# A windowed-attention and token-mixing kernel: the written-out order of all its work, replaced by a newly searched one

## The chip, the cores and the metric

One core of a Trainium2 chip. The metric is the time of one execution on the device, in microseconds (us), of which the median over runs is given. The engines that matter are TensorE (PE, with its weight loads PEld), VectorE (DVE), ScalarE (ACT), GpSimd (POOL) and the queue SP, which issues the DMA transfers. Each engine works through its own list of instructions in order and waits on semaphores for the others.

## The reference

Two branches work on the same x of 2048 tokens by 512 features, and a gate mixes them.

```python
x = A_x
g = sigmoid((x * gate_w).sum(-1, keepdims=True))
# A: attention, 32 heads of 16, each token sees itself and the 255 before it
q, k, v = split(x @ wqkv)
p = softmax(where(0 <= i - j < 256, q @ k.T / 4, -1e9))
a = (p @ v).reshape(S, D) @ wo
# B: layernorm over features, then an MLP over the tokens
h = layernorm(B_x)                      # B_x holds the same x here
u = gelu(h.T @ w1 + b1)                 # 512 x 1376
b = (u @ w2 + b2).T                     # 2048 x 512
out = g * a + (1 - g) * b
```

Scores, exponentials and products are in bfloat16 with sums in float32.

## The kernel before

**Tiles.** The tokens stand in 16 tiles of 128 (j = 0 to 15); scores are worked on in blocks of 128 queries that start half a tile late, so that a window of 256 needs two full blocks of keys (A, B) and two half-size corners (C).

**Tasks.** The program first writes down 1115 tasks. A task has a name, the engines that may run it with a cost in us for each, the tasks it waits for, and the buffers it takes and gives back. The names say what they do; a point and a number count pieces of one chain of matmuls:

- `q`, `k`, `v`: projections. `k3_2` is key group 3 of the third quarter of the tokens; `v12` is the values of tile 12. `qc`, `kc`, `vc` copy them out of PSUM. The quarters of x arrive transposed: the first by TensorE (`xta`, copied by `xtc`), the others by transposing DMAs (`xt1`, `xt2`, `xt3`).
- `s10.v1`: a score visit, 8 or 16 matmuls of 32 rows (line L942) into two pairs of PSUM banks; `s10.C`: a corner visit (L1043). `e10.v1.0` is ACT's exponential of one pair (L894), `m10.v1.0` its mask, a multiplication on DVE (L907, L974) or a selection on POOL (L536). `pv10.0` to `.3` multiply by the values (L1088), with four column tiles of 32. `n110`, `n210`, `nz10`, `n310`, `n410` normalise on DVE and put the result back into `xo`.
- `bs`, `ba`, `pow`, `h`: layernorm. `u0` to `u10`: the first layer of the MLP in chunks of 128 of the 1376; `ub` adds the bias. `gelu` is one task on ACT that works on all of u in four slices, between two loads of ACT's function table. `y0` to `y15`: the second layer and, as its last four matmuls, the output projection of the attention, in one accumulation; `f` applies gate and bias, `o` writes out.
- On SP: `x`, `wqk`, `wv`, `w1`, `w2`, `wo` load; `vs` and `vz` copy pieces of v to other partitions, so they wait for `vc`.

**What sets the order.** `PLAN` (L190) holds one string for each engine: the names in the order in which this engine runs them. After a colon stand the places of the buffers that a task takes, such as the two PSUM bank pairs of a score visit. So both which engine does a task and when is written out, and nothing moves at run time. A task whose turn has come holds up everything behind it on its engine.

`arrange` (L85) walks through these lists with the costs and gives each task a planned start. The plan is emitted in the order of these starts; they decide little else: a few waits between DVE and POOL where both use a port close in time, and the emission of a DMA among the others.

**Tiling of TensorE.** The array works either whole, or split into tiles of fewer rows or columns: mode `d` whole, `s` 32 by 128 (score visits), `c` 32 by 64 (corners), `p` 128 by 32 (products with the values), `h` 64 by 32. Pieces of the chains `q`, `k`, `v`, `u`, `y` are flexible: behind a task named in `THEN` they are written as four column tiles each, in mode `p`, and otherwise whole. Every piece of a chain is two matmuls of 512 columns, or eight when split.

Of the kernel before, what the change touches and what calls it, by code (L numbers as in the profile page):

```python
# [78 lines left out]
SWITCH = 0.095  # L79

BLOCK, AHEAD, FETCH, BUSY = 256, 80, 3.6, 3.0
LATENCY = {"PE": 0.22, "ACT": 0.15, "DVE": 0.12, "POOL": 0.15, "SP": 2.0}


def arrange(tasks):  # L85
# [21 lines left out]
    while len(order) < len(tasks):  # L107
# [19 lines left out]
        t.cost = t.engines[e]  # L127
        ins = t.ins
        if e == "PE":
            new = then if t.flex else t.mode  # L130
            if new != mode:
                t.cost += SWITCH
            if t.flex and new == "p":
                t.tiled = True
                ins *= 4
            if t.mode != "d":
                then = "p" if t.name in THEN else "d"
            mode = new
# [52 lines left out]
        warm:3 xta0.0.0:7 xta0.0.1:6 warmb xta0.1.1:4 xta0.1.0:5 q1_0.0:2 k3_0.0:3 k1_0.0:6 q3_0.0:1 k0_0.0:7  # L191
        q3_0.1 q0_0.0:0 k3_0.1 q1_0.1 q1_0.2 k1_0.1 k3_0.2 k0_0.1 q0_0.1 q2_0.0:5 q1_0.3 q0_0.2 q1_0.4 q0_0.3
        k3_0.3 q3_0.2 q0_0.4 k3_0.4 q3_0.3 k2_0.0:4 q2_0.1 k0_0.2 k1_0.2 k1_0.3 k0_0.3 k1_0.4 q2_0.2 q3_0.4 q2_0.3
        k0_0.4 k2_0.1 k2_0.2 k2_0.3 k2_0.4 q2_0.4 s0.v0:62 q3_1.0:0 q3_1.2 k3_1.0:1 k3_1.2 q0_1.0:7 s0.C:42 v1.0:6
        q0_1.2 s-1.C:02 v1.2 v2.0:5 v2.2 s1.v3:02 biast:4 v0.0:7 v0.2 v3.0:5 v3.2 q1_1.0:4 s1.v0:62 v5.0:1 q1_1.2
        gate0:5 v5.2 v14.0:0 s0.v1:62 v13.0:5 k2_1.0:1 v14.2 pv-1.0:6 v10.0:4 k2_1.2 v13.2 s1.v2:26 k2_2.0:0 v10.2
        v15.0:1 v12.0:5 v12.2 v15.2 k2_2.2 pv0.0:2 pv0.1 s1.v1:64 pv0.2 v4.0:1 v4.2 k3_2.0:0 k3_2.2 s2.v1:26 v7.0:5
        v7.2 k0_2.0:4 s1.C:60 k0_2.2 v6.0:3 v6.2 s2.v3:06 k0_1.0:2 k0_1.2 k1_1.0:5 k1_1.2 pv1.0:6 pv1.1 pv1.2
        s2.v0:02 v11.0:4 v11.2 v8.0:5 v8.2 pv1.3 pv1.4 s2.v2:20 q2_1.0:5 v9.0:4 q2_1.2 s2.C:26 v9.2 k1_2.0:1 k1_2.2
        u3.0:0 u3.2 s3.v1:64 u3.4 u3.6 u3.8 s3.C:26 u3.10 u3.12 u3.14 u2.0:1 s3.v2:24 pv2.0:6 pv2.1 u7.0:0 pv2.2  # L200
        pv2.3 u7.2 u2.2 s3.v0:42 u2.4 u7.4 u7.6 s3.v3:46 u7.8 u7.10 u7.12 s4.v0:62 u2.6 u2.8 u2.10 u2.12 u2.14
        s4.v1:24 pv3.0:6 pv3.1 pv3.2 pv3.3 u7.14 u10.0:1 u10.2 s5.v2:42 u10.4 u10.6 u10.8 s4.v3:62 u10.10 q0_2.0:0
        q0_2.2 s4.v2:64 u10.12 u10.14 q3_2.0:2 u0.0:3 q3_2.2 s4.C:06 u0.2 u0.4 u0.6 s6.v0:40 u0.8 u0.10 u0.12
        u6.0:2 u0.14 s5.v0:06 pv4.0:4 pv4.1 pv4.2 pv4.3 u6.2 u6.4 q2_2.0:3 s5.v1:06 u6.6 q2_2.2 u6.8 s5.C:64 u6.10
        u6.12 u5.0:3 s6.C:60 u6.14 u5.2 u5.4 s6.v2:46 u5.6 k3_3.0:2 k3_3.2 q1_2.0:1 q1_2.2 u5.8 s5.v3:46 u5.10
        u1.0:2 u1.2 s6.v1:06 u1.4 pv5.0:4 u5.12 pv5.1 pv5.2 pv5.3 s6.v3:06 u1.6 u5.14 u1.8 s7.v0:64 u1.10 pv6.0:0
        pv6.1 pv6.2 u1.12 pv6.3 s7.v1:64 u1.14 u4.0:3 u4.2 s7.v3:06 u4.4 k1_3.0:2 k1_3.2 s7.C:04 u4.6 u4.8 q0_3.0:2
        s7.v2:60 q0_3.2 u4.10 u4.12 u4.14 s8.v3:46 u9.0:2 u9.2 u9.4 s8.C:04 u8.0:3 u8.2 u8.4 u8.6 s8.v1:46 u8.8
        u9.6 u9.8 s8.v0:04 u8.10 u9.10 u9.12 u8.12 u8.14 s8.v2:06 pv7.0:4 u9.14 pv7.1 pv7.2 pv7.3 s10.v0:02
        k0_3.0:7 k0_3.2 q1_3.0:4 q1_3.2 q3_3.0:6 k2_3.0:5 k2_3.2 q3_3.2 pv8.0:0 pv8.1 pv8.2 pv8.3 y4.0:3 q2_3.0:6  # L210
        q2_3.2 y0.0:7 y0.2 y0.4 y8.0:2 y0.6 y4.2 y0.8 s9.v1:40 y4.4 y8.2 y0.10 y8.4 y0.11 y0.13 s9.v3:40 y4.6 y4.8
        y4.10 y4.11 s9.v2:60 y4.13 y8.6 y8.8 s9.C:04 y7.0:3 y8.10 y7.2 y8.11 s9.v0:60 y7.4 y8.13 y7.6 s10.C:46 y7.8
        y2.0:2 y2.2 s10.v3:06 y2.4 y7.10 y2.6 y7.11 s11.v3:46 y2.8 y7.13 pv9.0:0 pv9.1 pv9.2 pv9.3 s10.v2:64 y2.10
        y2.11 y9.0:3 y9.2 s10.v1:04 y2.13 y9.4 y9.6 s11.C:60 y9.8 y1.0:2 y1.2 s11.v2:40 y1.4 y1.6 y9.10 y1.8
        s11.v1:06 y9.11 y9.13 y1.10 y1.11 s13.v3:04 y1.13 pv10.0:6 pv10.1 pv10.2 pv10.3 s12.v2:02 y5.0:5 y10.0:4
        y10.2 s12.v0:26 y5.2 y10.4 y5.4 y10.6 s11.v0:06 y5.6 y5.8 y5.10 y5.11 s12.v1:02 y10.8 y10.10 y10.11 y5.13
        s12.v3:62 y10.13 pv11.0:0 pv11.1 pv11.2 y3.0:5 pv11.3 s13.v0:26 y3.2 y11.0:4 y11.2 s12.C:60 y3.4 y11.4
        y11.6 s13.C:62 y11.8 y11.10 y11.11 y3.6 s13.v1:20 y11.13 pv12.0:6 y3.8 pv12.1 pv12.2 pv12.3 s14.v3:20 y3.10
        y3.11 y6.0:4 y3.13 s13.v2:26 y6.2 y6.4 y12.0:5 s14.v2:06 y12.2 y12.4 y6.6 s14.v0:02 y6.8 y6.10 pv13.0:6
        pv13.1 pv13.2 y6.11 pv13.3 s14.v1:02 y12.6 y12.8 y6.13 s14.C:26 y12.10 y12.11 y12.13 y13.0:0 y14.0:1 y14.2  # L220
        y13.2 s15.A:62 pv14.0:4 pv14.1 y14.4 pv14.2 pv14.3 y13.4 s15.C:26 y14.6 y13.6 y13.8 s15.B:42 y15l.0:7 y14.8
        y15l.2 y15r.0:6 y15l.4 y15l.6 y13.10 pv15.0:4 y14.10 pv15.1 pv15.2 y15r.2 y15l.8 y15l.10 y15r.4 y13.11
        y14.11 y14.13 y13.13 y15r.6 y15r.8 y15l.11 y15l.13 y15r.10 y15r.11 y15r.13
    """,
    ACT="""
        xtc0.0.1 xtc0.1.0 xtc0.1.1 kc3_0 kc1_0 kc0_0 kc2_0 e0.v0.0:4 e0.v0.1:5 kc3_1 e0.C.1:8 e0.C.0:a e-1.C.1:7
        e-1.C.0:b vc1 vc2 e1.v3.1:2 e1.v3.0:3 vc3 e1.v0.0:6 e1.v0.1:9 vc5 gatee0 e0.v1.0:d e0.v1.1:c vc14 kc2_1
        vc13 e1.v2.1:b e1.v2.0:7 vc12 vc15 kc2_2 e1.v1.0:5 e1.v1.1:a vc4 e2.v1.1:4 e2.v1.0:8 e1.C.1:d e1.C.0:c vc7
        vc6 e2.v3.1:1 e2.v3.0:0 kc1_1 e2.v0.1:a e2.v0.0:9 vc8 vc11 e2.v2.0:b e2.v2.1:5 e2.C.1:e vc9 e2.C.0:f
        e3.v1.0:c e3.v1.1:d e3.C.0:7 e3.C.1:6 ub3 e3.v2.0:a e3.v2.1:4 e3.v0.0:b e3.v0.1:5 e3.v3.1:f e3.v3.0:e  # L230
        e4.v0.1:1 e4.v0.0:0 e4.v1.0:b e4.v1.1:4 ub7 e5.v2.1:f e5.v2.0:e e4.v3.0:a e4.v3.1:d e4.v2.0:5 ub10
        e4.v2.1:c e4.C.0:2 e4.C.1:3 e6.v0.1:9 e6.v0.0:8 gatee1 e5.v0.1:0 e5.v0.0:1 e5.v1.1:c e5.v1.0:d e5.C.0:4
        e5.C.1:5 e6.C.0:7 e6.C.1:6 e6.v2.1:a e6.v2.0:b kc3_3 e5.v3.1:g e5.v3.0:h e6.v1.0:2 e6.v1.1:3 gatee2
        e6.v3.1:g e6.v3.0:h e7.v0.0:f e7.v0.1:e ub5 e7.v1.0:g e7.v1.1:d e7.v3.0:h e7.v3.1:c e7.C.0:9 e7.C.1:8
        e7.v2.0:a e7.v2.1:b e8.v3.0:6 e8.v3.1:7 e8.C.1:3 e8.C.0:4 e8.v1.0:2 e8.v1.1:5 e8.v0.0:1 e8.v0.1:0 gatee3
        e8.v2.0:f e8.v2.1:e e10.v0.0:g e10.v0.1:h gelu e9.v1.1:b e9.v1.0:8 e9.v3.1:9 e9.v3.0:2 e9.v2.1:4 e9.v2.0:3
        e9.C.0:5 e9.C.1:i e9.v0.0:a e9.v0.1:j e10.C.1:6 e10.C.0:f e10.v3.1:0 e10.v3.0:c e11.v3.0:1 e11.v3.1:d
        e10.v2.1:7 e10.v2.0:e e10.v1.0:5 e10.v1.1:4 e11.C.1:3 e11.C.0:j e11.v2.1:b e11.v2.0:a e11.v1.0:i e11.v1.1:2
        e13.v3.0:9 e13.v3.1:8 e12.v2.1:c e12.v2.0:0 e12.v0.1:f e12.v0.0:g e11.v0.0:5 e11.v0.1:e e12.v1.1:4
        e12.v1.0:7 e12.v3.0:h e12.v3.1:e e13.v0.1:d e13.v0.0:6 e12.C.0:1 e12.C.1:j e13.C.1:3 e13.C.0:i e13.v1.0:5  # L240
        e13.v1.1:2 e14.v3.0:j e14.v3.1:b e13.v2.1:c e13.v2.0:f e14.v2.0:e e14.v2.1:a e14.v0.1:7 e14.v0.0:d
        e14.v1.1:h e14.v1.0:i e14.C.0:f e14.C.1:g f12:0 e15.A.1:c e15.A.0:h e15.C.0:j e15.C.1:5 e15.B.0:9 e15.B.1:f
        f14:1 f15l:3
    """,
    DVE="""
        const zeros bs3:1 xtc0.0.0 bs2:0 ba3 parity bs1:1 ba2 ba1 bs0:0 ba0 qc1_0 bs4:1 qc0_0 ba4 qc3_0 qc2_0 qc3_1
        bs8:1 bs9:0 qc0_1 ba8 ba9 bs11:1 biasc vc0 bs5:0 ba11 ba5 bs10:1 bs7:0 ba10 ba7 gatem0 bs14:1 qc1_1 bs6:0
        n1-1:0 ba14 h2 n2-1 ba6 ez0 vc10 nz-1:0 bs12:1 n3-1:1 ba12 bs15:0 n10:0 h11 kc3_2 ba15 n20 h4 bs13:1 nz0:1
        h5 ba13 n30:0 h8 h1 m1.C.1 kc0_1 kc0_2 h6 h3 m1.C.0 h13 h14 h9 h7 n11:2 h10 h12 h0 h15 qc2_1 gl12 n21
        m2.C.1 kc1_2 m2.C.0 m2.v1.1 gl5 gl14 m3.C.0 gl15 n12:8 gl7 m3.v0.0 n22 m3.C.1 m3.v0.1 gl13 m3.v3.0 gl6 ub2  # L250
        gl10 gl4 nz2:0 nz1:1 n13:6 gatem1 gl8 gl11 gl9 n40 n4-1 qc0_2 n31:1 n32:0 qc3_2 m4.C.0 m4.C.1 n41 ub0 ez1
        n23 n14:2 m5.v0.0 nz3:1 m6.v0.1 qc2_2 m5.v2.1 n33:1 n24 m5.v0.1 gatem2 nz4:0 ub6 m5.C.1 m5.C.0 m5.v1.0 n43
# [36 lines left out]
def kernel(  # L289
# [139 lines left out]
    def add(*a, **k):  # L429
        tasks.append(Task(*a, **k))  # L430
        return tasks[-1]
# [944 lines left out]
```

## Time and profile before

| what | value |
|---|---|
| median of 3 runs | 200.1 us (199.95 to 200.97) |
| profiled execution: span from first to last instruction | 198.5 us |
| granted TensorE clock | 0.999 |
| matmuls | 4058 |
| PE busy | 193.7 us |
| ACT busy | 169.2 us |
| DVE busy | 156.5 us |
| POOL busy | 79.9 us |

The profile has the span alone; the runs are measured from outside, and their median lies 1.6 us above it. A row of a group or of the timeline has the line, the engine, the operation, what it writes and reads by the program's names, and how many instructions there were. `pb` is a single PSUM bank, `ps` a pair; `et` and `XT` hold exponentials (the latter in the space of the transposed x once it is used up), `wb` the weights of the MLP, `xo` x and later the attention's result. PE's ends are modelled, so the distance from one start to the next says more than the length of a row. Numbers in brackets behind a row are the idle time ahead of it, and who ended it.

### The profile page before, as it was taken

What the parts mean: (1) busy time and instruction counts of PE and PEld (TensorE: products, weight loads), DVE (VectorE), ACT (ScalarE), POOL (GpSimd) and SP (SyncE); (2) the same over time, 40 slices, a digit from 0 to 9 for tenths busy, and PEclk for the clock granted to TensorE, in tenths of its full rate; (3) what the DMA queues carried; (4) which work ended last, traced back from release to release, by engine and by line L of the source; (5) the groups of instructions that cost most, each with busy time, mean ns of one, the idle gap of its engine ahead of it and who ended that gap; (6) DMA issues with size and microseconds to landing.
All of it is one profiled execution on the core that took longest, in us unless ns stands there. A gap on an engine that the chain in (4) does not pass through costs nothing. (4 is left out here: it accounts for less than half of the span.)

```text
span 198.5 us, 9100 instructions
## 1 busy us (share of the span) xinstructions
PE 193.7 (98%) x4058; PEld 93.9 (47%) x4058; DVE 156.5 (79%) x318; ACT 169.2 (85%) x198; POOL 79.9 (40%) x118
## 2 busy tenths in 40 slices
PE   7999999999999999999999999999999999999993
PEld 3644444354535435446534554344445354554572
DVE  1799888879998988986689789636767868869683
ACT  2369999999987996998999899899899989898632
POOL 6394897425334440213223200055069335561310
PEclk9999999999999999999999999999999999999999
DMA  5999799990060000001499870000202220200002
GB/s 159 293 286 227 112 295 268 360 223 1 8 174 20 15 0 3 3 5 32 120 344 385 275 193 3 26 26 30 75 30 71 47 69 21 62 30 29 30 7 79
DMA packets 23189, 22.02 MB, mean 111 GB/s; under 512 B 7566, under 2 KB 21262, under 8 KB 23150
## 3 DMA queue, kind: packets, MB, share of 16 engines
q1 hardware_dynamic: 23150, 21.44, 38.3%
q8 instruction: 32, 0.52, 1.2%
q14 instruction: 7, 0.06, 0.1%
HBM read 15.61 MB, written 2.10 MB: 89 GB/s over the span
## 5 line engine op out<-in xcount | busy, mean ns | idle before, releaser
L894 ACT ACTIVATE et<-ps 128x1024 bf16<-128x1024 f32 (+1 forms) x94 | 89.4, 1013 | 6.1 <-PE ps L942 2.2
L536 POOL TENSOR_SCALAR_AFFINE_SELECT et<-et 128x512 bf16<-128x512 bf16 (+2 forms) x63 | 46.6, 751 | 56.0 <-ACT et L894 40.9
L894 ACT ACTIVATE XT<-ps 128x1024 bf16<-128x1024 f32 (+1 forms) x60 | 58.2, 1010 | 7.6 <-PE ps L942 4.4
L670 PEld LDWEIGHTS <-wb 128*32 128x32 bf16 (+4 forms) x645 | 32.0, 97 | 34.5 <-issue 6.5
L670 PE MATMUL pb<-ug,wb 128*32 128x512 bf16 (+4 forms) x385 | 45.6, 366 | 0.0
L670 PE MATMUL pb<-h,wb 128*128 128x512 bf16 (+2 forms) x260 | 44.5, 381 | 0.0
L536 POOL TENSOR_SCALAR_AFFINE_SELECT XT<-XT 128x512 bf16<-128x512 bf16 (+1 forms) x28 | 20.0, 720 | 46.8 <-ACT XT L894 27.8
L670 PE MATMUL pb<-XT,wqkv 128*128 128x512 bf16 (+2 forms) x190 | 32.8, 374 | 0.2 <-ACT XT L894 0.2
L1179 DVE STREAM_TRANSPOSE et<-ps 128x1024 f32<-128x1024 f32 (+1 forms) x17 | 20.1, 1183 | 12.0 <-PE ps L1088 11.3
L1088 PEld LDWEIGHTS <-VA 128*32 128x32 bf16 (+1 forms) x1056 | 20.1, 97 | 6.5 <-issue 1.3
L942 PE MATMUL ps<-QZ,KT 32*128 32x256 bf16 (+1 forms) x496 | 23.1, 265 | 0.0
L754 DVE TENSOR_TENSOR QZ<-pb,par 128x1024 bf16<-128x1024 f32 x16 | 19.5, 1219 | 3.2 <-PE pb L670 3.1
L670 PEld LDWEIGHTS <-wqkv 128*128 128x128 bf16 (+1 forms) x190 | 12.9, 99 | 14.3 <-ACT XT L894 0.5
L670 PE MATMUL pb<-wo,xo 128*32 128x512 bf16 (+2 forms) x152 | 18.0, 375 | 0.0
L1088 PE MATMUL ps<-et,VA 128*32 128x128 bf16 (+2 forms) x624 | 17.9, 218 | 0.0
L942 PEld LDWEIGHTS <-KT 32*128 32x128 bf16 x496 | 7.4, 92 | 20.6 <-ACT et L894 10.6
L670 PE MATMUL pb<-wqkv,XT 128*128 128x512 bf16 (+1 forms) x70 | 16.5, 381 | 0.0
L974 DVE TENSOR_TENSOR et<-et,mask 128x512 bf16<-128x512 bf16 x26 | 13.3, 510 | 2.5 <-ACT et L894 2.4
L441 DVE TENSOR_SCALAR ot<-pb,c,c 128x512 bf16<-128x512 f32 (+1 forms) x11 | 8.6, 783 | 7.4 <-PE pb L670 7.4
L1088 PE MATMUL ps<-XT,VA 128*32 128x128 bf16 (+2 forms) x432 | 13.9, 215 | 0.0
L1088 PEld LDWEIGHTS <-VZ 128*32 128x32 bf16 x832 | 13.2, 98 | 0.7
L770 DVE BATCH_NORM_STATS2 stats<-xo 128x6 f32<-128x512 bf16 x16 | 10.7, 682 | 3.1 <-DMA xo<-in_A_x_dram 3.1
(76 smaller groups left out, 200.1 us busy)
## 6 DMA issues: line engine op xcount, KB each, us to landing
wb<-in_B_w_dram SPq DMA_DIRECT2D x8, 512.0 KB, 7.6
wb<-in_B_w_dram SPq DMA_DIRECT2D x2, 2048.0 KB, 9.2
VZ<-VA SPq DMA_DIRECT2D x26, 70.0 KB, 2.7
xo<-in_A_x_dram SPq DMA_DIRECT2D x3, 512.0 KB, 6.3
out_dram<-ot SPq DMA_DIRECT2D x12, 128.0 KB, 2.0
wb<-in_B_w_dram SPq DMA_DIRECT2D x4, 352.0 KB, 5.9
wqkv<-in_A_wqkv_dram SPq DMA_DIRECT2D x4, 256.0 KB, 5.2
wb<-in_B_w_dram SPq DMA_DIRECT2D x1, 1024.0 KB, 5.3
```

Of the source, the lines that this page charges most:

```text
L441: return nc.vector.tensor_scalar(out=out_, in0=in_, scalar1=scale, scalar2=bias, op0=ALU.mult, op1=ALU.add)
L536: return nc.gpsimd.affine_select(out=out_, in_=in_, pattern=[[0, n] for n in pattern] + [[step, HB]], compare_op=op, fill=0.0, base=base_, ...
L670: made.append(nc.tensor.matmul(buf(b)[c:z_, c0:c0 + w_], lhsT=lhsT[:, c:z_], rhs=rhs, start=(j == 0), stop=(j == n - 1), skip_group_check= ...
L754: lambda k=k, b=b: nc.vector.tensor_tensor(out=QZ[:, k, :, (i % NQ) * SB:(i % NQ + 1) * SB], in0=buf(b)[:, None, :].to_broadcast([P, 2, SB ...
L770: f"bs{t_}", {"DVE": 0.67}, lambda b=b, t_=t_: nc.vector.bn_stats(buf(b)[:], xo[:, t_, :]),
L894: lambda e=e, b=b, shape=shape: nc.scalar.activation(out=shape(buf(e)), in_=shape(buf(b)), func=ACT.Exp, scale=SCALE),
L942: made.append(nc.tensor.matmul(to[:, :, done:done + m], lhsT=keys(j if x == "A" else j - 1, k)[rows], rhs=q[rows], start=True, stop=True, ...
L974: made.append(nc.vector.tensor_tensor(out=v, in0=v, in1=m.to_broadcast(list(v.shape)), op=ALU.mult))
L1088: return lambda: nc.tensor.matmul(to(), lhsT=v() if callable(v) else v, rhs=buf(e)[rows, col:col + n], start=first, stop=last, tile_positi ...
L1179: lambda: nc.vector.transpose(out=view(buf(tr).bitcast(FP32)), in_=view(buf(o))), [last], takes=[tr], uses=[o],
```

## The change

Two things change together.

The first is the costs in `arrange`: one price for every change of tiling becomes a table by kind, and a function corrects the costs of operations. The latencies, the time of an instruction fetch and the cost of `gelu` are lowered.

```diff
-SWITCH = 0.095
-BLOCK, AHEAD, FETCH, BUSY = 256, 80, 3.6, 3.0
-LATENCY = {"PE": 0.22, "ACT": 0.15, "DVE": 0.12, "POOL": 0.15, "SP": 2.0}
+TURN = {
+    "d": dict(d=0, s=0.100, p=0.100, c=0.098, h=0.100),
+    "s": dict(d=0.116, s=0, p=0.115, c=0.105, h=0.114),
+    "p": dict(d=0.134, s=0.116, p=0, c=0.110, h=0.130),
+    "c": dict(d=0.172, s=0.160, p=0.169, c=0, h=0.160),
+    "h": dict(d=0.150, s=0.137, p=0.135, c=0.140, h=0),
+}
+BLOCK, AHEAD, FETCH, BUSY = 256, 80, 2.8, 1.5
+LATENCY = {"PE": 0.21, "ACT": 0.15, "DVE": 0.11, "POOL": 0.12, "SP": 2.0}
+
+def cost_of(t, e):
+    c, n = t.engines[e], t.name
+    if e == "PE":
+        return c - 0.02 if t.mode == "s" else c * 0.738 if t.mode == "c" else c
+    if e == "DVE":
+        return max(0.1, c - 0.06)
+    if e == "ACT":
+        return c - 0.085 if n[:2] in ("vc", "kc", "ub") else c - 0.008 if n[0] == "e" else c
+    if e == "POOL" and n[0] == "m" and ".C" in n:
+        return c * 1.14
+    return c
...
-        t.cost = t.engines[e]
+        t.cost = cost_of(t, e)
...
-            if new != mode:
-                t.cost += SWITCH
+            t.cost += TURN[mode][new]
...
-    gelu = add("gelu", {"ACT": 8.3}, emit_gelu, ub)
+    gelu = add("gelu", {"ACT": 7.0}, emit_gelu, ub)
```

The second is the five lists of `PLAN` and the set `THEN`, all written anew. The operations are the same 1115 tasks. 41 masks go from POOL to DVE and 25 from DVE to POOL; 8 copies and the like go from DVE to ACT and 10 the other way. From the lists, the stretches that the prediction speaks of (old, then new):

```diff
 PE, around the transposed third quarter of x
-  gate0:5 v5.2 v14.0:0 s0.v1:62 v13.0:5 k2_1.0:1 v14.2 pv-1.0:6 v10.0:4 k2_1.2 v13.2 s1.v2:26 k2_2.0:0 v10.2
+  q1_1.2 v14.0:1 v14.2 s1.v0:26 gate0:5 v3.0:0 v2.0:4 v2.2 k3_1.0:1 v3.2 pv-1.0:2 s0.v1:64 k3_1.2
+  k3_2.0:0 k3_2.2 q0_1.0:3 v13.0:2 q0_1.2 s1.v2:46 v13.2 v12.0:0 v10.0:1 v10.2 v12.2 pv0.0:4 pv0.1
 PE, around the gelu
-  s10.v0:02 k0_3.0:7 k0_3.2 q1_3.0:4 q1_3.2 q3_3.0:6 k2_3.0:5 k2_3.2 q3_3.2 pv8.0:0 pv8.1 pv8.2 pv8.3 y4.0:3
-  q2_3.0:6 q2_3.2 y0.0:7 y0.2 y0.4 y8.0:2 y0.6 y4.2 y0.8 s9.v1:40 y4.4 y8.2 y0.10 y8.4 y0.11 y0.13 s9.v3:40
+  s10.v0:06 k0_3.0:3 k2_3.0:2 k2_3.2 pv8.0:0 pv8.1 pv8.2 pv8.3 s9.v1:46 q3_3.0:2 q3_3.2 k0_3.2 q1_3.0:0
+  q2_3.0:1 q1_3.2 q2_3.2 y4.0:2 y0.0:3 y0.2 y0.4 y0.6 y0.8 y0.10 y0.11 y4.2 y4.4 s9.v3:04 y0.13 y4.6 y4.8
+  s9.v2:46 y2.0:3 y2.2 y2.4 s9.C:04 y2.6 y2.8 y4.10 y4.11 s9.v0:06 y4.13 y2.10 y2.11 y2.13 s10.C:04
 ACT, around the gelu
-  e8.v2.0:f e8.v2.1:e e10.v0.0:g e10.v0.1:h gelu e9.v1.1:b e9.v1.0:8 e9.v3.1:9 e9.v3.0:2
+  ub9 e8.v2.1:1 e8.v2.0:d e10.v0.0:0 e10.v0.1:7 gelu e9.v1.0:d e9.v1.1:1 e9.v3.1:c e9.v3.0:g
 DVE, start and early part
-  const zeros bs3:1 xtc0.0.0 bs2:0 ...
+  zeros bs1:0 ba1 const bs0:0 xtc0.1.0 ba0 ... n2-1 ez0 ba6 bs13:1 bs15:0 ba13 qc0_1 bs14:1 ...
 SP, loads
-  x0.0 x0.2 wqk0 wqk1 wqk2 wqk3 x1.4 xt1 wv x2.8 bias xt3 x3.12 xt2 vs0 w1_02 w1_03 vs1 w1_22 vs2 gw w1_12
-  w1_23 w1_01 w1_00 w1_10 w1_11 vz2:0 w1_13 vz3:1 vz4:2 vz5:0 w1_20 w1_21 vz6:1 vz8:0 w2_0 vz7:2 w2_1 w2_2
+  x0.0 x0.2 wqk0 wqk1 wqk2 wqk3 x1.4 xt1 wv bias x2.8 xt3 vs0 x3.12 xt2 vs1 w1_13 vz2:0 vs2 w1_10 gw
+  vz3:2 w1_01 w1_23 w1_02 w1_11 w1_03 w1_12 w1_00 w1_21 vz4:1 w1_20 vz6:0 w1_22 vz8:2 wo vz5:1 vz7:1
+  w2_0 w2_1 vz9:0 w2_2 ...
 end of ACT and of DVE
-  ACT: e15.B.0:9 e15.B.1:f f14:1 f15l:3        DVE: n315:1 n415 f13:2 f15r:0
+  ACT: e15.B.0:d e15.B.1:f f13:0                DVE: n315:0 n415 f14:1 f15l:0 f15r:3
```

## The prediction

> **What bounds the kernel now.** I read the page's busy shares first, then busy time by stage, then the chain of waits, and last the timelines of ScalarE and of the SP queue around two places that the new order touches.
>
> The page's first part and two of its strips of 40 slices:
>
> ```profile
> PE 193.7 (98%) x4058; PEld 93.9 (47%) x4058; DVE 156.5 (79%) x318; ACT 169.2 (85%) x198; POOL 79.9 (40%) x118
> ...
> PE   7999999999999999999999999999999999999993
> ...
> PEclk9999999999999999999999999999999999999999
> ```
>
> TensorE is the bound at full clock from the first projection to the end. Busy time by stage (window and its length, then busy us of each engine):
>
> ```profile
> 6.10:46.00 39.90, 39.90 (x538) 17.81 (x537) 34.49 (x83) 34.36 (x51) 24.98 (x34) 1.00 0.99 250
> 46.00:113.00 67.00, 67.00 (x1518) 32.18 (x1516) 57.36 (x119) 61.02 (x71) 22.55 (x33) 1.00 0.29 95
> 113.00:137.00 24.00, 23.82 (x356) 10.35 (x344) 18.16 (x37) 22.74 (x23) 5.38 (x7) 1.00 0.26 78
> 137.00:186.00 49.00, 48.94 (x1412) 24.90 (x1415) 36.13 (x60) 44.59 (x48) 21.44 (x27) 1.00 0.16 47
> ```
>
> PE has no hole anywhere; ACT (fourth busy figure) is the runner-up, and in 113 to 137, where the gelu stands, it fills 22.74 of 24.00. "Busy" hides small losses, since pipelined matmuls overlap, so I look at starts. The chain of waits gives them (start, length, what):
>
> ```profile
> 163.84 0.38 PE ps L1043 x32
> ...
> 166.01 1.63 PE pb L670 x27
> 167.64 0.33 PE ps L942 x8
> ...
> 172.59 1.40 PE pb L670 x6
> 173.99 0.33 PE ps L942 x8
> ...
> 180.36 0.67 PE ps L1043 x32
> 181.03 2.91 PE pb L670 x13
> ```
>
> Thirteen chain matmuls take 2.91, six 1.40: (2.91 - 1.40)/7 = 0.216 each. Six are then 1.295, and the 0.105 left over is the change of tiling into the score visit behind them. The run of 27 instructions is seven chain matmuls, most of them split in four column tiles: 1.63 - 7 x 0.216 = 0.12, so a split piece costs what a whole one does. Going through all PE pieces from first matmul to first matmul, a change costs 0.093 to 0.106 for most kinds, and 0.185 on leaving a 32x64 corner visit (c). The order has 169 changes, 18.7 us in all. From 6.13 us to the end the remainder is 168.3 of work, about 0.55 of half-speed matmuls before 7.2 us, about 0.7 of dust of 0.01 us a piece, and true stalls of only 1.0: 0.25 and 0.08 at 113.0 to 114.5, 0.13 ahead of the corner visit at 143.6, 0.285 in the one at 180.36 (0.67 where its like takes 0.38), 0.25 in scraps. So no better order can win more than the changes it saves plus about 1 us.
>
> **What the skill says.** The Trainium skill, "TensorEngine Tiling (Array Packing)", Key Properties, states that changing the tiling mode drains TensorE. The trace agrees and prices it (0.1 a change); the forecast goes by the trace. "ScalarE: Activation LUTs", What ACT_TABLE_LOAD costs, puts a load of a function table at about 2.7 us; this trace shows 1.28 us twice, and I go by 1.28.
>
> **The change, part by part.**
>
> Changes of tiling. In the new PE list, with its set of tiled chain pieces, they fall from 169 to 161. By kind (d whole array, s score visit, c corner visit, p column-tiled, h 64-row): c to d +2, c to p -2, d to c +4, d to p -4, d to s +1, p to c -4, p to d -3, p to h -1, p to s -1, s to d +2, s to h +1, s to p -3. With the medians: 0.00 + 0.00 + 0.10 - 0.42 - 0.32 - 0.12 - 0.11 + 0.21 + 0.10 - 0.31 = -0.85 us. Tiled chain pieces fall from 74 to 65, matmuls from 4058 to 3988; by the row above that is worth nothing. The matrix work is identical, all on the path: -0.85.
>
> Stalls of the old order. The 0.33 at 113 goes with the order that caused it (pieces k0_3 and q1_3 waited for banks); the 0.13 and the 0.285 stand at places that the new order lays otherwise. I count -0.75 and keep the scraps.
>
> The gelu. The planner's figure goes from 8.3 to 7.0. ACT's timeline:
>
> ```profile
> 111.59 3.88 ACT L894 ACTIVATE XT<-ps 128x1024 bf16<-128x1024 f32 x4 [0.83 <-ACT ez L837]
> 115.50 1.28 ACT L1254 ACT_TABLE_LOAD   x1
> 116.79 4.66 ACT L1254 ACTIVATE ug<-ug 128x1536 bf16<-128x1536 bf16 x3
> 121.36 0.61 ACT L1256 ACTIVATE ug<-ug 96x512 bf16<-96x512 bf16 x1
> 121.99 1.28 ACT L894 ACT_TABLE_LOAD   x1
> 123.59 1.94 ACT L894 ACTIVATE et<-ps 128x1024 bf16<-128x1024 f32 x2 [0.32 <-PE ps L942]
> ```
>
> From the last exponential (115.48) ACT can do the next at 123.27: 7.8 us, two table loads included. The old figure was 0.5 too long, so ACT even waited 0.32; the new one is 0.8 too short. Laid out by hand from the start of visit s10.v0 (zero): the visit 0.33, its two exponentials end at 2.36 (0.92 apart, 1.02 long), the gelu's slices are out at 5.1, 6.9, 8.3 and 8.8, the exponentials start again at 10.15, and the first ends at 11.2. PE meanwhile does s10.v0, three k pieces, pv8 (1.36), s9.v1 and seven projection pieces, is at y4.0 at 6.4, at y0.6 at 8.15 (needs slice three: +0.2), and would be at s9.v3 at 10.8, whose pair of banks the first exponential frees at 11.2: +0.4. The next two visits, s9.v2 and s9.C, wait for banks freed by exponentials 0.92 apart and lose 0.1 each; from s9.v0 on PE is behind ACT. Sum +0.8; bounds 0.3 (the freed banks come early) and 1.1 (ACT reaches the gelu late by the 0.3 it was behind at 113).
>
> Masks. 41 mask multiplications go from GpSimd to VectorE and 25 the other way: 16 more on DVE, at 0.34 to 0.6 apart some 6.5 us, beside 156.5. Over the run it stays under PE. In 6 to 46, six of them (+2.0) and one net copy (+0.6) lift DVE from 34.5 to about 37 of 39.9. There qc0_1, behind layernorm statistics on DVE, comes about 0.15 late for visit s1.v1. With the many other inputs that now arrive within 0.1 us of their use I take +0.3 for new waits outside the gelu; bounds 0 and 1.0.
>
> SP's queue. The last transposed load of x (xt2) moves behind vs0, which waits for the copy of v tile 0 (about 18.2). Two copies (1.2) and x3 (0.6) later it is issued at 20.0, against 16.6 before; its first user, k3_2, moves up: adding PE's pieces at their traced lengths in the new order puts it at 26.3; in the old one k2_2 was first, at 28.1. The rows (issue time and duration; time to landing):
>
> ```profile
> 15.99 0.58 SPq L454 DMA_DIRECT2D xo<-in_A_x_dram  x1
> 16.62 5.76 SPq L463 DMA_TRANSPOSE XT<-in_A_x_dram  x1
> ...
> DMA to landing us min/median/max: 5.4/7.7/7.8
> ```
>
> It lands at 25.4 to 27.8. Each of the three landed about 1.85 after the x load ahead of it, and x3, issued at 19.4, now meets empty engines (estimate from the first x load, 2.9 for half the bytes: landing near 23), so I take the early end and 0; the late one costs 1.4. The w1 loads also leave later, behind vz2 and vs2; at the earlier pace the last of their first group lands near 43.5, against u3 at 46.5: covered by about 3 us. The w2 loads keep 1 us of cover before y4.0.
>
> Start and end. "zeros" ahead of "const" starts the warming matmuls 0.17 earlier, but the transposes still wait for x (xta at 3.77): 0. At the end f15l moves to DVE ahead of f15r; it starts 0.55 before f15r's input is ready and is 0.54 long: 0, at most 0.2.
>
> Sum against the profiled execution: -0.85 - 0.75 + 0.8 + 0.3 = -0.5, span 198.5 to 198.0. The runs' median 200.1 is 1.6 above that span; this stays, so **199.6 us**.
>
> **Rivals.**
>
> *A smooth order.* Exponentials are back in time and nothing new waits: -0.85 - 0.75 + 0.3 = -1.3, 198.8. For it: PE never waited long before, and DVE and ACT have room over the run. Against: 22.74 of 24.00 in the gelu's stage.
>
> *The transposed load is late (slower).* If xt2 takes 7.8 us as it did before, k3_2 stalls 1.4 on the one queue that PE cannot work round, on top of the main case: +0.9, 201.0; with the upper bounds of the waits (1.1 and 1.0) 202.0. It decides from a landing at about 27.5. For it: the row of 5.76. Against: x3 before it was itself held up then.
>
> *Margins gone.* The planner's costs of DVE, ACT and latencies all shrink to what single rows show, so every small delay shows: waits of 1.0 in place of 0.3, 200.3: no change.
>
> *It does not do what it says*: the changes saved are real, but ACT sets the pace in the gelu's stage, so all 0.85 comes back there as waiting: 200.4.
>
> **How the numbers follow.** 0.5% is 1.0 us, about what a measurement of this kernel can tell from no change: the three runs spread by as much. Main case 45% (range 199.1 to 200.2), smooth 22%, margins gone or ACT's pace 20%, late load 13%. The smooth case lies mostly below 199.1, the main case's lower edge a little: faster 0.25. The late load lies half over 201.1, and so does the upper edge of lost margins: slower 0.12. Same 0.63. The range from 198.5 (smooth, with 0.3 more) to 201.1 leaves out half of the late load and little else.
>
> **What would show it.** 3988 matmuls and no PE hole longer than about 0.5; after the second table load the first exponential starts without idle time, and the score visits just after it wait for ACT's exponentials, 0.8 in sum; the first use of XT at about 26.5 without a wait for a DMA. The forecast is wrong if PE waits for the transposed load, if visits wait for masks on DVE throughout, or if the visits after the gelu find their banks free.

## The result and the profile after

| | before | after |
|---|---|---|
| median of 6 runs | 200.2 us (199.95 to 200.97) | 203.57 us (202.8 to 204.32) |
| span of the profiled execution | 198.5 | 202.6 |
| start of the last matmul | 195.2 | 199.2 |

The changed kernel takes 1.016 times as long (95% interval 1.0138 to 1.0182). The prediction was 199.6 with a range of 198.5 to 201.1: the wrong side, and outside.

The page of the changed kernel, with the lines that answer to those shown of before and the one on instruction transfers:

```profile
PE 195.0 (96%) x3988; PEld 93.7 (46%) x3988; DVE 156.1 (77%) x336; ACT 168.2 (83%) x196; POOL 65.4 (32%) x100
...
PE   7999999999999999999999689999999999999993
...
PEclk9999999999999999999999969999999999999999
...
q8 instruction: 31, 0.51, 1.1%
```

PE was 9 throughout before; now it has a 6 and an 8 beside each other, and the granted clock a 6 in the slice of the 8. Busy time by stage (window and length, then PE, PEld, DVE, ACT, POOL, clock, DMA share, GB/s):

```profile
6.10:46.00 39.90, 39.79 (x520) 17.75 (x521) 36.42 (x88) 33.67 (x49) 22.44 (x32) 1.00 0.90 253
46.00:113.00 67.00, 67.00 (x1545) 32.12 (x1542) 57.58 (x133) 60.88 (x70) 16.81 (x23) 1.00 0.29 95
113.00:138.00 25.00, 22.52 (x329) 9.84 (x326) 15.43 (x25) 21.45 (x21) 5.50 (x7) 0.93 0.21 70
138.00:190.00 52.00, 51.72 (x1267) 24.60 (x1269) 35.23 (x70) 46.80 (x52) 15.51 (x22) 1.00 0.13 37
```

Most of it is lost in the gelu's stage, and there PE, ACT and DVE are all idle more than before. The chain of waits has the place (start, length, what), with one later spot:

```profile
113.10 1.41 PE pb L696 x24
114.51 0.30 PE ps L1114 x22
114.81 2.48 issue
117.28 1.31 PE ps L1114 x106
...
166.61 0.35 PE ps L1069 x23
166.96 0.27 issue
167.23 0.32 PE ps L1069 x9
```

PE stops in the middle of pv8, between two matmuls of the same kind, and the chain names no engine and no DMA that released it: "issue". The same in the middle of corner visit s12.C. From the row ahead of the hole to the row behind it 2.66 us pass beyond the usual distance; the chain's 2.48 goes by a modelled end. Before, the stretch ahead of pv8 and its first pieces were (PE's timeline; the second row is the start of pv8):

```profile
113.59 3.72 PE L670 MATMUL pb<-XT,wqkv 128*128 128x512 bf16 x16 [0.18 <-ACT XT L894]
117.24 0.46 PE L1088 MATMUL ps<-et,VA 128*32 128x128 bf16 x20
```

Sixteen whole matmuls stood there for 3.7 us; now there are 24 column-tiled ones for 1.41. Stretches of 1 us around the first hole in the new order:

```profile
114.00:115.00 1.00, 0.81 (x34) 0.36 (x25) 0.96 (x3) 1.00 (x2) 0.00 (x0) 1.00 1.11 442
115.00:116.00 1.00, 0.00 (x0) 0.00 (x0) 0.25 (x1) 0.98 (x2) 0.00 (x0) 1.00 1.00 279
116.00:117.00 1.00, 0.00 (x0) 0.00 (x0) 0.00 (x0) 0.99 (x2) 0.00 (x0) 1.00 0.30 78
117.00:118.00 1.00, 0.71 (x68) 0.72 (x72) 0.00 (x0) 1.00 (x2) 0.00 (x0) 1.00 0.02 8
118.00:119.00 1.00, 1.00 (x64) 0.56 (x50) 0.29 (x1) 1.00 (x1) 0.00 (x0) 0.68 0.08 16
119.00:120.00 1.00, 1.00 (x7) 0.38 (x4) 1.00 (x2) 1.00 (x2) 0.00 (x0) 0.50 0.00 0
```

For most of the wait the DMA engines are full (share 1.11 and 1.00), and 1.1 us after PE has gone on, its clock falls to half until 121.8.

**What PE waited for.** I numbered PE's rows in the trace, matmuls, weight loads and the sequencer's own together. Every hole of this kind, in the traces of before, after and experiments 1 to 5, ends exactly at a row whose number is 193 more than a multiple of 256. (The traces of experiments 6 to 9 lack some 20 to 30 matmul records, so their rows can't be numbered.) And the trace's instruction queue (q8) carries one packet of 16 KB for each 256 rows: 31 packets for 8014 rows. So I take these for the blocks of PE's own program; experiments 1 and 4 test it. The packet for the next block starts, with few exceptions, after the current one has been entered, and where PE stands waiting for it the first row runs 1.3 to 1.5 us after the packet's end:

| (us) | block entered | its successor's packet | took | last row before the next block | next block's first row |
|---|---|---|---|---|---|
| before, at pv8 | 112.11 | 113.79 | 0.98 | 117.57 | 117.58 |
| after, pv8 | 111.80 | 114.99 | 0.97 | 114.61 | **117.28** |
| after, s12.C | 163.77 | 164.48 | 1.38 | 166.75 | **167.23** |
| after, pv15 | 191.43 | 192.46 | 1.05 | 194.36 | **194.81** |
| before, visit at 180.36 | 177.34 | 178.31 | 0.98 | 180.51 | **180.72** |

Without loads, 3.0 to 3.6 us pass from entering a block to the first possible row of the next (in experiment 4 also 2.5 and 2.7, where the packet began within 0.4); at pv8 it was 5.5, since the packet started 3.2 us after the block had been entered. The two loads of the last part of w2 had been issued at 110.59 and 111.68. How long 256 rows last depends on what they are: a whole chain piece is 4 rows for 0.43 us, a column-tiled one 16 rows in the same time, and pv8.1 is 96 rows in 0.45. Before, eight whole projection pieces (32 rows, 3.5 us) stood ahead of pv8, and the block lasted 5.5 us; the new order has three there, column-tiled, and the 256 rows were over in 2.8.

**Where the 4.1 us come from.** PE's time beyond the usual length of its pieces, after 6 us, is 2.3 before and 7.3 after. Of the 7.3, 2.66 are the hole in pv8, 1.54 the half-speed clock behind it, 0.55 and 0.49 the fetches in s12.C and pv15, and 0.22 a hole in visit s4.v3 at 66.09, at the first row of a block too; the packet for that one had ended 2.2 us before, so what held PE there is open. The other 1.8 answer to 2.1 before. With -0.85 for the changes of tiling that is 7.3 - 2.3 - 0.85 = 4.1, the difference of the spans. The clock fell in two of the six runs (mean granted clock 0.992, spans 202.6 and 202.4, against 1.000 and 201.1 to 202.3 in the other four), so the half-speed stretch is a part of the profiled execution's loss that most runs did not have.

### The profile page after: what moved, and what is told of

The parts are those of the page before. It is cut to its first block, busy times and chain, and to the rows that moved or that the text cites. A ratio compares the mean times of both kernels' runs of the same rounds, so it can differ in the third digit from the quotient of the medians.

```text
span 202.6 us, 8943 instructions
## 1 busy us (share of the span) xinstructions
PE 195.0 (96%) x3988; PEld 93.7 (46%) x3988; DVE 156.1 (77%) x336; ACT 168.2 (83%) x196; POOL 65.4 (32%) x100
## 4 chain that ended last, share of the span: by engine, by line
PE 94%; issue 2%; DMA 1%; DVE 1%
PE pb L696 69%; PE ps L1114 11%; PE ps L968 10%; PE ps L1069 3%; DMA xo<-in_A_x_dram 1%; PE pb L634 1%; DVE stats L796 1%; DVE XT L629 0%; PE ps L1024 0%; PE pb L617 0%; DVE junk L467 0%; PE pb L828 0%; DVE mv L800 0%; PE pb L582 0%
## 5 line engine op out<-in xcount | busy, mean ns | idle before, releaser
L920 ACT ACTIVATE et<-ps 128x1024 bf16<-128x1024 f32 (+1 forms) x107 | 101.4, 1011 | 7.9 <-PE ps L968 4.2
L562 POOL TENSOR_SCALAR_AFFINE_SELECT et<-et 128x512 bf16<-128x512 bf16 (+3 forms) x57 | 41.9, 745 | 59.4 <-ACT et L920 29.8
L920 ACT ACTIVATE XT<-ps 128x1024 bf16<-128x1024 f32 (+1 forms) x47 | 45.4, 1014 | 6.9 <-PE ps L968 6.3
L696 PE MATMUL pb<-ug,wb 128*128 128x512 bf16 (+3 forms) x307 | 44.6, 373 | 0.0
L696 PE MATMUL pb<-h,wb 128*32 128x512 bf16 (+2 forms) x298 | 43.9, 380 | 0.0
L562 POOL TENSOR_SCALAR_AFFINE_SELECT XT<-XT 128x512 bf16<-128x512 bf16 x16 | 10.4, 660 | 60.4 <-ACT XT L920 27.8
L1000 DVE TENSOR_TENSOR et<-et,mask 128x512 bf16<-128x512 bf16 x41 | 16.9, 421 | 6.7 <-ACT et L920 6.6
L1205 DVE STREAM_TRANSPOSE et<-ps 128x1024 f32<-128x1024 f32 (+1 forms) x11 | 13.2, 1201 | 7.3 <-PE ps L1114 2.6
L696 PE MATMUL pb<-wqkv,XT 128*128 128x512 bf16 x64 | 16.9, 381 | 0.0
L933 DVE TENSOR_TENSOR et<-et,mask 128x1024 bf16<-128x1024 bf16 (+1 forms) x16 | 10.3, 648 | 3.8 <-ACT et L920 3.8
```

The source lines that it names most:

```text
L562: return nc.gpsimd.affine_select(out=out_, in_=in_, pattern=[[0, n] for n in pattern] + [[step, HB]], compare_op=op, fill=0.0, base=base_, ...
L696: made.append(nc.tensor.matmul(buf(b)[c:z_, c0:c0 + w_], lhsT=lhsT[:, c:z_], rhs=rhs, start=(j == 0), stop=(j == n - 1), skip_group_check= ...
L920: lambda e=e, b=b, shape=shape: nc.scalar.activation(out=shape(buf(e)), in_=shape(buf(b)), func=ACT.Exp, scale=SCALE),
L933: return nc.vector.tensor_tensor(out=v, in0=v, in1=m[:, None, :].to_broadcast([P, n, w]), op=ALU.mult)
L1000: made.append(nc.vector.tensor_tensor(out=v, in0=v, in1=m.to_broadcast(list(v.shape)), op=ALU.mult))
L1205: lambda: nc.vector.transpose(out=view(buf(tr).bitcast(FP32)), in_=view(buf(o))), [last], takes=[tr], uses=[o],
```

## The experiments

**1. Without the load beside it.** The last of the w2 loads is all but left out, so the second layer's sums are not those of the reference.

```diff
-            nc.sync.dma_start(w2[:, lo:hi, :], B_w2[lo * P:hi * P, :].rearrange("(t p) s -> p t s", p=P))
             if hi == full_:
-                nc.sync.dma_start(w2[:F - full_ * P, full_, :], B_w2[full_ * P:F, :])
+                nc.sync.dma_start(w2[:F - full_ * P, full_, 1536:], B_w2[full_ * P:F, 1536:])
+                return
+            nc.sync.dma_start(w2[:, lo:hi, :], B_w2[lo * P:hi * P, :].rearrange("(t p) s -> p t s", p=P))
```

> The changed kernel without nearly all of the third load of w2 (1.0 MB and three quarters of 384 KB are left out, so rows 1024 and up of w2 hold stale data). Theory F (an instruction fetch of TensorE waits behind this load, and the next 256 rows are used up too soon): TensorE reaches the block's end at about 114.6 as before, the fetch that began at 115.0 begins at about 112.5, and the hole of 2.66 us in pv8 shrinks to 0 to 0.5 us, with no half-speed stretch behind it; the profile's span falls from 202.6 to 199 to 200. Then the gelu's lateness on ScalarE is uncovered: about 0.8 us of waits of the score visits after it. Rival D (the hole comes from too many instructions in too short a time, whatever the load): the hole stays above 1.5 us. Rival W (pv8 waits for a mask or an exponential): the hole stays at 2.66 us.

The packet started 0.85 after its block was entered (113.94, 114.79), took 0.94, and the hole shrank from 2.66 to 0.22. The chain of this run:

```profile
116.65 0.30 PE ps L1114 x22
116.95 0.04 issue
116.98 1.26 PE ps L1114 x106
...
120.01 3.27 ACT ug L1280 x2
123.28 0.52 ACT ug L1282
123.80 0.02 issue
123.81 1.28 ACT L920
125.10 0.01 issue
125.11 1.03 ACT XT L920
126.14 0.04 issue
126.19 0.40 PE ps L968 x8
```

The load made the fetch late; that is shown: the rivals that lay the hole on the number of rows alone, or on a mask or an exponential, expected over 1.5. And the wait that the prediction had put here now comes out: behind pv8 the chain runs over the gelu's slices, the second table load and the first exponential into visit s9.v3 (126.19), which lost 0.45, and the two after it 0.10 each: 0.65 in place of my 0.8. In the changed kernel the hole had hidden it, because PE came too late to find ACT behind. The span is 201.7 all the same, where I had expected 199 to 200, since this one execution began badly: the first projection at 7.07 in place of 6.04, at half speed until 10.4, some 2 us.

**2. The costs alone.** The new price table and function with the old `PLAN` and `THEN`.

> The new costs in the planner with the old lists and the old set of tiled pieces. Theory F and all others that lay the loss on the order: same as before, 200.2 us within 0.3, since each engine's order is written out and the costs move only the emission among engines. Rival C (the planned starts matter, by the waits between GpSimd and VectorE that hang on them): a difference of over 0.5 us, in waits of POOL.

200.67 us over 20 runs, ratio 1.0014 (1.0002 to 1.0026), span 198.7. The new costs by themselves change next to nothing (0.1%); the loss is in the lists. It also gives a check on the planner: for this pair of order and prices `arrange` puts the last PE work at 194.9 (trace 195.35), for the changed kernel at 193.2 (trace 199.24). It was right to half a microsecond on the old order, and wrong by six on the one that had been searched with its prices.

`arrange` can also say which of the lowered prices hid the loss. This is its arithmetic and no run. With the two figures of the fetch alone put back to 3.6 and 3.0, and all else of the changed kernel kept, it ends the new order at 200.8 and leaves the old one at 194.9; with the gelu alone put back to 8.3 it ends the new order at 194.4. So at the old price of the fetch the planner would have refused this order by 5.9 us, though it lays the waits only in part where the trace has them.

**3. The projections ahead of pv8.** The four key and query groups go back in front of pv8 (other banks, copies on DVE in the matching order), and `k0_3` and `k2_3` are no longer column-tiled.

```diff
-  k0_3.0:3 k2_3.0:2 k2_3.2 pv8.0:0 pv8.1 pv8.2 pv8.3 s9.v1:46 q3_3.0:2 q3_3.2 k0_3.2 q1_3.0:0 q2_3.0:1 q1_3.2 q2_3.2
+  k0_3.0:3 k2_3.0:2 k2_3.2 k0_3.2 q3_3.0:4 q3_3.2 q1_3.0:5 q1_3.2 q2_3.0:3 q2_3.2 pv8.0:0 pv8.1 pv8.2 pv8.3
-  y4.0:2 y0.0:3 y0.2 y0.4 y0.6 y0.8 y0.10
+  y4.0:2 y0.0:3 y0.2 y0.4 y0.6 y0.8 s9.v1:46 y0.10
```

> The changed kernel with the seven projection pieces k0_3.2, q3_3, q1_3, q2_3 ahead of pv8 instead of behind it, whole instead of tiled, on other PSUM banks, and visit s9.v1 later. All work is done. Theory F: TensorE reaches the end of its block of 256 rows about 3 us later, at 117.4, when the fetch is there, so hole and half-speed stretch are gone: 203.6 falls to about 200.0 to 201.0, with 0.3 to 0.8 us of waits after the gelu showing now. Rival G (the gelu's cost is the main loss): nothing is gained but a few tenths, 203 or more.

202.2 us, ratio 1.009 (1.0058 to 1.0122), spans 200.1 to 201.6. No hole in pv8 and no half-speed clock, worth 1.4 us by the medians. The rest was taken at the next places: 0.59 in y0.6 (block entered at 118.50, packet 119.15, 1.12 long, next block at 121.77 with its row before at 120.98), 0.56 in s12.v2 just ahead of y5.2, 0.60 in pv15, all three at the first row of a block, and again the gelu, 0.91 at s9.v3. I had expected 200.0 to 201.0: the holes moved on and did not go away. The experiment moves the pieces and leaves them whole at once, so it does not tell the two apart.

**4. The same order, 80 rows on.** Five warming matmuls of 512 columns become 45 of 56.

```diff
-    add("warm", {"PE": 2.2}, lambda: warming(5, 512), [kz], takes=[wu], ins=10)
+    add("warm", {"PE": 2.2}, lambda: warming(45, 56), [kz], takes=[wu], ins=90)
```

> The changed order with nothing moved: only the five warming matmuls of 512 columns at the start, whose result nobody uses, become 45 of 56 columns, so that PE's instruction list is 80 rows longer ahead of everything else at about the same time. If PE waits for the next 256 rows of its own program, the places where it can wait are set by the count of rows and move 80 rows forward in the work: no hole between pv8.1 and pv8.2 (2.66 us before), but one in or at k0_3.0, just behind visit s10.v0. There the block before is entered at about 111.2 and 5.5 us later, the delay measured beside the load w2_2, is 116.7, where PE would have been at 113.25: about 3.5 us (2.7 to 4.0). The next place is then in pv8.3, 256 rows and 2.3 us of work on, with another 0.7 to 1.5. The hole of 0.55 in s12.C goes or moves into pv11.3, the one in pv15 into pv15.0. Span 203 to 206. If instead the hole belongs to what pv8 reads, to its banks, or to the order around it, it stays between pv8.1 and pv8.2 at 2.7 and the span stays near 202.6.

209.63 us in one run, span 207.9. The hole between pv8.1 and pv8.2 is gone (0.08), and every place that the row count had named shows one: k0_3.0 (0.30), pv8.3, pv11.3 (1.49) and pv15.0 (0.13). Three that I had not named, s7.v1 (1.19), pv10.3 (0.5) and y11.13 (0.5), end at the first row of a block as well. Their sizes I had the wrong way round: the packet at k0_3.0 started at once, within 0.02, and the one for pv8.3 2.5 us late, so the long one, 2.88, is in pv8.3. The span lies above my 203 to 206. The chain, first k0_3.0, then pv8.3:

```profile
116.53 0.12 issue
116.64 1.10 PE pb L696 x17
117.75 1.34 PE ps L1114 x89
119.09 2.65 issue
121.74 0.35 PE ps L1114 x18
122.09 0.33 PE ps L968 x8
122.42 4.60 PE pb L696 x13
```

Nothing was moved in the order of the work, so operands, banks and neighbours of pv8 are out; only the count of rows ahead of it changed, and the start, which came later. Behind the 2.88 the clock fell to half again (122.8 to 126.2), behind 1.49 and 1.19 not. Some 1.9 of the loss are at the start: with the many small warming matmuls PE was at half speed until 10.2.

**5. A new order with the fetch priced.** I searched again, from the old order, with the changed kernel's prices but other figures for the fetch and the gelu.

> An order of all tasks searched from the old one, with the changed kernel's prices for operations, changes of tiling and latencies, but with the fetch of 256 rows of PE's program at 3.15 us, 2.9 more while w2 is being loaded, blocks counted from row 193, and the gelu at 7.8. Part of the search's weight lies on a set of prices that is worse in all of these. By the same arithmetic the old order has its last PE work at 195.6 (traced: 195.35) and this one at 194.2. Theory (the new prices are right but for the fetch and the gelu): last PE row near 193.9, span near 197.3, no PE hole over 0.5 anywhere, ratio to the kernel before 0.993 (0.988 to 0.998). Rival (the close prices of copies, masks and latencies are what costs, through many small waits): this order uses the same prices and ends like the changed kernel, span 200 or more, ratio 1.005 to 1.02.

204.0 us, span 202.8, ratio 1.0156 (1.0104 to 1.0207): a miss. The rival's numbers came out (over 200, 1.005 to 1.02), but not its many small waits. Beside w2 no hole is left, and one fetch elsewhere cost 0.48 (next block at 42.10; its packet started 5.6 us after the block before was entered, while w1 came in). The loss is one hole of 2.82 ahead of y1.0, and 1.3 of half-speed clock behind it:

```profile
143.64 0.45 SPq L1322
144.09 0.04 issue
144.14 4.11 DMA out_dram<-ot
148.25 0.03 issue
148.28 0.02 DVEq L457
148.30 0.05 issue
148.35 0.82 DVE ot L457
149.17 0.05 issue
149.21 2.74 PE pb L686 x6
```

y1.0 waits for its bank, the bank for an output on DVE, that for the buffer of an earlier output, and this for its store, 4.6 us from issue to landing. The planner's figure for a store is 2.0 behind its issue.

**6 and 7. Stores priced too.** Two seeds.

> As in the run before, an order searched from the old one with the changed kernel's prices for operations, changes of tiling and latencies, the fetch at 3.2 (2.6 more beside w2, 2.5 more in the first 45 us), the gelu at 7.9; and now the landing of an output store at 4.2 us behind its issue in place of 2.0, since the run before lost 2.8 us and a half-speed clock at y1.0 to a bank held by an output that waited for a store. By the same arithmetic the old order has its last PE work at 195.5 (traced: 195.35) and this one at 194.3; with all prices raised 201.5 and 196.1. Theory: only these three prices (fetch, gelu, store) were wrong in the changed kernel's planner: no PE hole over 0.6, no half-speed clock, last PE row 194 to 195, span 197.3 to 198.3, ratio 0.990 to 0.999. Rival (the close prices of copies, masks and latencies are what costs): holes in other places, span 200 or more, ratio over 1.004.

> A second order from the same search and prices with another seed, to see whether the arithmetic holds for more than one order: last PE work at 194.6 by the sum (196.8 with all prices raised). Theory: no PE hole over 0.6, last PE row 194.3 to 195.3, span 197.6 to 198.6, ratio 0.992 to 1.000. Rival: as in the run with the first seed, ratio over 1.004.

201.65 us, ratio 1.0067 (1.002 to 1.0114), and 201.61, 1.0068 (1.0044 to 1.0092): no fetch hole, no store, no half-speed clock, and still over the old order, on the rival's side of 1.004 (spans 199.4 and 199.9). Both traces have about 1.0 at visit s9.v3, which is over the 0.6 that I had allowed. PE's visit s9.v1 and then ACT's timeline, of the first:

```profile
123.08 0.40 PE L958 MATMUL ps<-QZ,KT 32*128 32x256 bf16 x8
...
117.01 4.66 ACT L1270 ACTIVATE ug<-ug 128x1536 bf16<-128x1536 bf16 x3
121.57 0.61 ACT L1272 ACTIVATE ug<-ug 96x512 bf16<-96x512 bf16 x1
123.56 1.28 ACT L910 ACT_TABLE_LOAD   x1 [1.38 <-DVE QZ L770]
124.86 1.02 ACT L910 ACTIVATE et<-ps 128x1024 bf16<-128x1024 f32 x1
```

ACT is free at 122.18 and its second table load starts at 123.56, 0.08 after visit s9.v1 has ended (123.08 + 0.40, a modelled end). The second seed and experiment 3 show the same (124.14 after 124.06, 123.66 after 123.58), while the load follows the gelu within 0.02 where that visit was done early, as in the kernel before. So in these traces the table load waits for the same scores as the exponential behind it, and counting it into the gelu was wrong: it belongs to the first exponential. The first seed also lost 0.6 at a copy of v that came by DMA later than its 2.0.

**8 and 9. The table load priced as part of the exponential, and the copies of v at 3.0.** Two seeds.

> Searched as before, with one more price. In the two orders before this one PE waited 0.9 at visit s9.v3 although 7.9 was planned for the gelu: ACT stood idle for 1.4 us ahead of its second table load, which started only when the visit before (s9.v1) had its scores ready. So the gelu is now 6.6, and 1.3 is put on the first exponential behind it; loads of v's copies by DMA land 3.0 behind their issue in place of 2.0. By this arithmetic the old order has its last PE work at 197.2 (traced 195.35, so it is about 1.9 too careful) and this one at 194.1. Theory (the order is better once fetch, gelu with its table load, stores and copies by DMA are priced): PE has no hole over 0.4, last PE row 192.8 to 194.5, span 196 to 198, ratio 0.983 to 0.997. Rival (something that no price holds turns up once more, as the store did): a hole of 0.7 or more in a new place, span 198.5 or more, ratio 1.000 to 1.01.

> The same prices, another seed, and started from the old order and not from the two orders before: last PE work at 194.6 by the sum. Theory: no PE hole over 0.4, span 196.3 to 198.3, ratio 0.985 to 0.998. Rival: a hole of 0.7 or more in a new place, ratio 1.000 to 1.01.

200.33 us, ratio 0.9992 (0.9971 to 1.0013), and 200.47, 1.001 (0.9994 to 1.0026). No hole over 0.4 behind the start in either; last PE row at 194.6 in the second against 195.2 before. In the first it is 195.5, with 1.1 lost to a late first weight load. Both ratios miss the theory's range and lie next to or in the rival's (1.000 to 1.01), without its new hole of 0.7, unless the late weight load counts as one. Against the old order nothing is lost now, and nothing is gained. These are new orders and not the changed one repaired, so they show that an order free of such holes is possible, and not that the changed order's loss was these holes alone. What remains open is where the rest of the promised gain goes; the runs don't tell a start that varies by some 1 us from many waits of 0.1. No order here beat the old one.

## Why the prediction was wrong, step by step

- *What bounds the kernel, and its stalls.* Right: PE, with 1 us of true stalls, and those at 113 and 143.6 did go with the old order. But the 0.285 in the visit at 180.36 was a fetch (the last row of the table above), and I put it down as a stall of the old order that goes with it. It was the one row of that trace that showed the missing mechanism, with its price: 3.4 us for 256 rows.
- *Changes of tiling, -0.85.* Right as far as can be seen: with it the two PE sums close to 0.1. (The ten terms as printed add up to -0.87.)
- *The fetch of PE's program, for which the sum has no term.* **This is the step that failed.** I put it at nothing and gave no reason. The diff lowers its price from 3.6 to 2.8, and from 3.0 to 1.5 extra beside a load; I set the cost of gelu, which the same diff lowers, against the trace, and not these. Measured, it is mostly 3.0 to 3.6 unloaded, and 5.5 beside w2: a hole of 2.66 us at pv8, 1.54 more by the clock, and 1.0 in s12.C and pv15. The one place where I looked at the number of instructions is *"Tiled chain pieces ... worth nothing"*: by the row of 27 instructions a split piece takes as long as a whole one, which is true, but it takes four times the rows, and I priced rows at nothing. (The planner counts a split piece's rows fourfold; the changed one also adds 0.0025 us for each row before splitting, a line that the diff above does not show.) At pv8 the splitting is the smaller part. Whole, the three pieces ahead of it would be 36 rows fewer, and 36 rows of pv8.1 take 0.17 us (an estimate from its 96 rows in 0.45). What brought the block's end forward is that five whole pieces of 0.43 went behind pv8. The Trainium skill, "Runtime: NRT & Kernel Launch", section "Instruction fetch mechanics", has the 256-instruction blocks, loaded by the engine's own queue, which fits the packets; it also holds that issue is slower than the fetch and so hides it, and there the measured 2.66 us stand against it.
- *"No PE hole longer than about 0.5".* Wrong: 2.66, and 1.54 more by the clock, which none of my cases had.
- *Gelu, +0.8.* Mechanism and place right, the size nearly: 0.65 without the hole, 1.1 in experiment 3 where s9.v1 comes later. In the changed kernel itself it costs nothing, because PE was late already.
- *xt2.* The early end was right: its packets ended at 24.6, and k3_2.0 (26.07) didn't wait. The rival with the late load is out.
- *Masks and new small waits, +0.3.* The scraps are 1.8 against 2.1, so no more than that; the rival of lost margins is out in this form. DVE in 6 to 46 rose to 36.4, where I had about 37; over the run its busy time stayed the same (156.1 against 156.5), where I had 6.5 more.
- *Start and end, 0.* The first score visit is 0.3 earlier in the profiled execution; the end is the same.
- *Rivals.* None named the fetch. All shared the assumption that PE's list costs only what its matmuls and its waits for other engines cost.

## What to carry to other kernels

An engine that bounds the kernel can wait for its own program. Count the instructions ahead of time, not only the microseconds: in these traces, where 256 rows of PE ran in less than about 3.4 us, or 5.5 while large loads were landing, there was a hole that no semaphore explains. What helps is long work of few rows in such a block, as the eight whole pieces were before. And when a search minimises a planner's sum, it finds the places where the planner is too cheap: here the fetch, then the store, then the table load came out one after the other, so check first the prices that were lowered, each against a row under load, and read the sum as right only near the order that it was fitted on.

## What was not expected of the hardware

- The start of an instruction packet depends on the load: mostly 0.3 to 1.6 us after its block is entered in quiet stretches (a few start up to 2.2 ahead of the first row), mostly 2.3 to 3.9 while x, w1 or w2 is landing, and 5.0 to 5.9 at one place in three traces (experiments 1, 3 and 5, some 40 us in); the packet itself mostly takes 0.9 to 1.5, up to 2.6.
- A pause of PE of 2.66 to 2.88 us was followed by half the granted clock for about 3.4 us (two of six runs of the changed kernel, experiments 4 and 5), beginning 1.1 us after PE had gone on in after and in experiment 4; 1.49 us was not. Stretches of experiment 5 (PE's figure first, the clock third from the end):

```profile
148.00:149.00 1.00, 0.00 (x0) 0.00 (x0) 0.65 (x1) 0.07 (x1) 0.00 (x0) 0.79 0.00 0
149.00:150.00 1.00, 0.79 (x2) 0.28 (x3) 1.00 (x3) 0.00 (x0) 0.38 (x1) 0.50 0.00 0
150.00:151.00 1.00, 1.00 (x4) 0.41 (x3) 1.00 (x3) 0.00 (x0) 1.00 (x2) 0.50 0.38 131
```

Here it begins 0.6 us before PE goes on (148.57 against 149.21). The Trainium skill, "TensorE: Matmul & The Clock Gate", section "Why this matters for your kernels", warns of pauses over some 3 us; in these runs less was enough.
- In experiment 5 a store of 128 KB, issued within 4 us behind four copies of v and another store on its queue, took 4.6 us from issue to landing; the median there was 2.7.
